# A head pair's keys, queries and values in one transfer each, and key remainders written across the halves

## The chip, the cores and the metric

One core of one Trainium2 chip runs one program. The metric is its device time in microseconds (us). The core has a matrix engine (PE, whose weight loads are shown as PEld), a vector engine (DVE), a scalar engine (ACT), GpSimd (POOL), and SyncE (SP), which here only issues transfers to one hardware queue that 16 DMA engines serve. Every engine works through its own instructions in order.

## The reference

Attention with a local window of 96 positions, 8 global keys and a linear distance bias, for 4 batches of 8 heads, 768 positions and width 64; then a two-layer block on 3072 tokens whose activation is h·cos(h). All in fp32.

```python
scores = scale * np.matmul(q, k.transpose(0, 1, 3, 2))          # q, k, v: 4 x 8 x 768 x 64
scores = np.where(keep, scores + bias, -1e9)                    # keep: last 96 positions, or the first 8 keys
a = np.exp(scores - scores.max(-1, keepdims=True))
a = a / (a.sum(-1, keepdims=True) + 1e-9)
x = np.matmul(a, v)                                             # then 3072 x 512
h = x @ w_in                                                    # 512 x 2048
return (h * np.cos(h)) @ w_out                                  # 2048 x 512
```

## The kernel before

The sequence is cut into blocks of 96 positions. A part is two to four such blocks of one batch: two parts of four blocks for the first batch, and parts of three, three and two blocks for each of the other three batches, 11 in all. A unit is one pair of heads of one part, so there are 44. The first eight units ("exact", parts 0 and 1) use q and k as they come: one transfer of 128 rows brings a pair (L626), the queries are scaled (L631, L633), and L676 makes the scores. The other 36 go through `plan_split`, once for each head: a number is cut into a high part that the fast matmul takes and a remainder. For that the head's 64 rows of keys and queries are brought twice, once into rows 0 to 63 and once into rows 64 to 127 of a `raw` buffer, each by its own transfer (L784). Then `qhigh` (L787, ACT) and `qrest` (L791, DVE) make both query parts on all 128 rows, `khigh` (a copy, line L308 on ACT, L310 on DVE, L312 on POOL) rounds the keys on all 128 rows, and `krest` (L801) overwrites rows 64 to 127 with the keys' remainder. So one matmul (L680) over 128 rows sums high and remainder. There are two `raw` buffers and two `qk` buffers, one per head of a pair.

The scores are folded and biased (L698, L707, DVE), go through exp (L732, ACT), are normed (L740, L743 on DVE; L760 and L765 on POOL or DVE), turned (L864, PE), copied (L308, L310, L875, L881) and multiplied with the values (L915, PE). The values of a unit come in two transfers: the blocks, 96 rows (L577), and the 8 global rows, broadcast to every block (L580); L838 makes the difference of neighbouring blocks. The products go into `xmem` as high part and remainder (L308, L963).

The two-layer block runs in steps: L998 multiplies by w_in; L1016, L1019, L1022, L1055 (L1121 in the first two parts) make h·cos(h); L1066 (L1129) and L1157 to L1169 make parts, remainders and sums; L1011 (first parts) or L1216 (others) multiplies by w_out. L1216 takes sums of w_out that were stored to DRAM earlier (L509 to L549) and are streamed back (`ws`, L1182, 256 transfers). The weights come as 64-bit words and are converted in the first 118 us (L441 to L478).

The order of everything is written by a planner in the kernel (`Plan`): each step has a cost in ns for each engine that may run it, a due time, the steps it waits for and the buffers it holds. The planner plays the whole kernel through, and always starts the ready step with the earliest due time; SP's transfers have a cost `extra` that stands for the queue's time, and SP stops issuing while more than 2.5 us of it are ahead. So a changed cost or a changed wait can re-order any engine's list. In the first 45 us of the plan it also puts idle matmuls (L1550) where it sees PE free.

Of the kernel before, what the change touches and what calls it, by code (L numbers as in the profile page):

```python
# [42 lines left out]
QS = KS + SW  # L43
# [17 lines left out]
NT, NST, NPV, NX, NV, NRAW, NQK, NRR, NG, NOO = 4, 3, 3, 3, 3, 2, 2, 3, 2, 2  # L61
# [222 lines left out]
class Net:  # L284
    def __init__(self, ctx, tc, qo, qk, qt, kt, v, lim, w_in, w_out, out):
        self.tc, self.nc = tc, tc.nc
        self.qo, self.qk, self.v, self.w_in, self.w_out, self.out = qo, qk, v, w_in, w_out, out
        self.qt, self.kt = qt, kt
        self.lims = lim
        self.B, self.S, _ = v.shape  # L290
        _, _, self.H, self.D, _ = qk.shape
# [267 lines left out]
    def plan_loads(self, n, b2):  # L559


        nc, p, D = self.nc, self.plan, self.D
        b, ts = self.parts[n]
        W = 2 * UB * D
        nb = len(ts)
        t0 = ts[0] * R
        lead = 1 if t0 == 0 else 0
        nt = 1 + nb - lead
        vs = Slot("v" if nt <= CT else "v5", lambda i: self.work.tile(
            [SLOT, CT + (i in self.plan.places["v5"]), W], F32, name="v", tag=i))  # L570
        low = lead if nb == CT else 0
        L = dict(n=n, first=t0 == 0, v=vs, nb=nb, low=low)
        src = self.v[b][:, b2 * W : (b2 + 1) * W]
        s = t0 - (1 - lead) * R

        def blocks(e):
            nc.sync.dma_start(vs.tile[:R, lead - low : lead - low + nt], src[s : s + nt * R].rearrange("(t p) d -> p t d", p=R))  # L577

        def glob(e):
            nc.sync.dma_start(  # L580
                vs.tile[R:, lead - low : nb - low], src[:G].rearrange("p (t d) -> p t d", t=1).broadcast_to([G, nb - lead, W])
            )
# [20 lines left out]
    def plan_unit(self, L, pr):  # L603
# [10 lines left out]
        early = n < len(OPEN)  # L614
# [4 lines left out]
        source = self.qo[n] if early else self.qk[(n - len(OPEN)) // len(BLOCKS), (n - len(OPEN)) % len(BLOCKS)]  # L619
        if exact:  # L620
            raw = Slot("early raw", lambda i: self.work.tile([P, QK if i == "raw0" else KS + 2 * SW], F32, name="raw", tag=i))
            src = source[2 * pr : 2 * pr + 2].rearrange("j p w -> (j p) w")
            kw = KW if early else KS
# [12 lines left out]
            ready = [p.op({ACT: 100 + wq * 420 // 384, DVE: 70 + wq * 230 // 384, POOL: 100 + wq * 390 // 384},  # L636
                          queries, [o], [raw], port=True)]
            heads = [(raw, ready)] * 2
        else:
            heads = [  # L640
                self.plan_split(source[2 * pr + j], k0, k1, wq, self.steepness(2 * pr + j)) for j in range(2)
            ]
# [19 lines left out]
        for job in jobs:  # L662
# [27 lines left out]
            ))  # L690
            so.slack = SLACK if n not in EARLY else 0
# [80 lines left out]
    def plan_split(self, src, k0, k1, wq, sc):  # L772
# [10 lines left out]
        def load(e, a):  # L783
            nc.sync.dma_start(raw.tile[a : a + D, k0 : KS + wq], src[:, k0 : KS + wq])  # L784

        def qhigh(e):
            nc.scalar.activation(qk.tile[0][:, 0, :wq], raw.tile[:, KS : KS + wq], AF.Copy, scale=sc)  # L787

        def qrest(e):
            qs = qk.tile[0]  # L790
            nc.vector.scalar_tensor_tensor(  # L791
                qs[:, 1, :wq], raw.tile[:, KS : KS + wq], sc, qs.bitcast(F32)[:, 0, :wq],
# [14 lines left out]
        q = self.chain("qhigh", p.op({ACT: 60 + wq * 350 // 384}, qhigh, loads, [raw, qk]))  # L807
        q = p.op({DVE: 70 + wq * 400 // 384}, qrest, [q], [raw, qk], port=True)
        k = self.chain("khigh", p.op(
            {ACT: 50 + w * 427 // 512, DVE: 70 + w * 265 // 512, POOL: 100 + w * 490 // 512},  # L810
            khigh, loads, [raw, qk], port=True,
        ))
        k = p.op({DVE: 70 + w * 535 // 512, POOL: 100 + w * 1125 // 512}, krest, [k], [raw, qk], port=True)
# [656 lines left out]
    def windows(self):  # L1470
# [8 lines left out]
                "tt": names("tt", NT), "st": names("st", NST), "qk": names("qk", NQK), "raw": names("raw", NRAW),  # L1479
# [9 lines left out]
        self.joined = []  # L1489
# [11 lines left out]
        self.when.pop()  # L1501
        self.xmem = self.const.tile([P, NX * 2 * self.NP * MW], F32R, name="xmem")
# [66 lines left out]
def layout(q, k, v, n_global, n_local, moe_w_in, moe_w_out):  # L1569
# [9 lines left out]
    def arrange(kt, qt, parts, kw, w):  # L1579
        qk = np.zeros((len(kt), len(parts), H, D, w), q.dtype)  # L1580
        for c, blocks in enumerate(parts):
            s0 = blocks[0] * R
            if c > 0:
                qk[:, c, :, :, :R] = kt[..., s0 - R : s0]
            for i, t in enumerate(blocks):
                s, o = t * R, (i + 1) * SLOT
                qk[:, c, :, :, o - G : o] = kt[..., :G]
                qk[:, c, :, :, o : o + R] = kt[..., s : s + R]
                qk[:, c, :, :, kw + i * R : kw + (i + 1) * R] = qt[..., s : s + R]
        return qk  # L1590
# [4 lines left out]
        qo=arrange(kt[:1], qt[:1], OPEN, KW, QK)[0],  # L1595
        qk=arrange(kt[1:], qt[1:], BLOCKS, KS, QS),
        qt=np.ascontiguousarray(qt),
        kt=np.ascontiguousarray(kt),
        v=np.ascontiguousarray(v.transpose(0, 2, 1, 3)).reshape(B, S, H * D),
        lim=np.concatenate([words(n_global).reshape(1), words(n_local).reshape(1)]),  # L1600
# [26 lines left out]
```

## Time and profile before

| what | value |
|---|---|
| device time, median of 3 runs | 683.9 us (682.43 to 684.13) |
| the profiled execution: its own time | 682.26 us |
| the profiled execution: its span (first to last instruction) | 679.8 us |
| PE, PEld, DVE, ACT, POOL busy | 662.9, 626.1, 567.7, 503.4, 372.5 us |
| granted TensorE clock, mean | 0.998 of full speed |
| moved by DMA | 136.69 MB in 86291 packets |

How to read it: the span is what the trace covers, and some 2.5 us of the run's time lie around it. Busy times of PE overlap, since its matmuls are pipelined; the wait of PEld or PE before an instruction is the better measure of what PE loses. DMA is read by the busy share of its 16 engines.

### The profile page before, as it was taken

How to read it: one execution, taken by the hardware profiler on the slowest of the kernel's cores; microseconds unless marked ns; L12 is line 12 of the kernel's file. 1: busy time of each engine (PE TensorE's matmuls, PEld its weight loads, DVE VectorE, ACT ScalarE, POOL GpSimd, SP SyncE). 2: the span in 40 equal slices, each digit the busy share in tenths (PEclk: the TensorE clock that was granted, in tenths of full speed). 3: DMA queues.
4: the chain of work that ended last, by engine and by line, in shares of the span. 5: the costliest groups of instructions: out<-in, count | busy, mean ns of one | idle time of the engine just before them, and what ended most of it. 6: DMA issues, size and time to landing. Idle time of an engine off the chain costs nothing.

```text
span 679.8 us, 17477 instructions
## 1 busy us (share of the span) xinstructions
PE 662.9 (98%) x5805; PEld 626.1 (92%) x5805; DVE 567.7 (84%) x1782; ACT 503.4 (74%) x1265; POOL 372.5 (55%) x526
## 2 busy tenths in 40 slices
PE   8998999999999999999999999999999999999995
PEld 4667999998999999999999999999999999999995
DVE  7889998989889878878889979887788988886764
ACT  7999999768786666877779769668678696673332
POOL 6675544347676646475755664555856565442301
PEclk9999999999999999999999999999999999999999
DMA  8999300053456476878778778777778877865664
GB/s 273 330 319 388 78 1 1 1 175 104 137 161 217 137 230 190 251 210 227 229 225 233 237 209 245 244 241 213 214 218 244 234 208 236 234 195 186 219 195 152
DMA packets 86291, 136.69 MB, mean 201 GB/s; under 512 B 9904, under 2 KB 33968, under 8 KB 86192
## 3 DMA queue, kind: packets, MB, share of 16 engines
q1 hardware_dynamic: 86048, 135.23, 65.1%
q8 instruction: 48, 0.79, 0.5%
q14 instruction: 51, 0.42, 0.2%
q10 hardware_dynamic: 144, 0.26, 0.1%
HBM read 118.67 MB, written 16.78 MB: 199 GB/s over the span
## 4 chain that ended last, share of the span: by engine, by line
PE 69%; ACT 12%; DVE 9%; DMA 5%; POOL 2%; issue 2%; SPq 0%; POOLq 0%; DVEq 0%; ACTq 0%
PE bank L998 30%; PE bank L1216 19%; PE bank L1011 8%; PE bank L680 5%; PE bank L915 5%; DMA raw<-in_qk_dram 2%; PE bank L864 2%; ACT raw L447 2%; ACT rr L1022 2%; ACT raw L463 1%; ACT w L308 1%; ACT tt L732 1%; DMA raw<-in_w_out_dram 1%; DVE rr L1055 1%; DMA raw<-in_w_in_dram 1%
## 5 line engine op out<-in xcount | busy, mean ns | idle before, releaser
L998 PE MATMUL bank<-xmem,w 128*128 128x256 f32 (+1 forms) x2112 | 347.2, 295 | 1.7 <-DVE rr L1055 0.9
L998 PEld LDWEIGHTS bank<-xmem,w 128*128 128x128 f32 x2112 | 294.6, 188 | 10.8 <-DVE rr L1121 1.6
L732 ACT ACTIVATE tt<-tt,st 96x104 f32<-96x104 f32 (+1 forms) x256 | 94.7, 371 | 13.1 <-DVE st L707 12.6
L1022 ACT ACTIVATE rr<-rr,half_pi 128x512 f32<-128x512 f32 (+1 forms) x104 | 72.2, 694 | 38.9 <-DVE rr L1019 38.4
L1011 PE MATMUL bank<-w,gh 128*128 128x256 f32 (+1 forms) x384 | 87.9, 319 | 0.0
L1016 ACT ACTIVATE rr<-bank 128x512 int32<-128x512 f32 (+1 forms) x104 | 58.3, 561 | 26.3 <-PE bank L998 26.1
L1216 PE MATMUL bank<-ws,sh 128*128 128x256 f32 x384 | 77.1, 285 | 0.3 <-DVE oo L1235 0.2
L1019 DVE SCALAR_TENSOR_TENSOR rr<-rr,bank 128x512 f32<-128x512 int32 (+1 forms) x104 | 66.2, 638 | 7.1 <-ACT rr L1016 7.0
L765 POOL TENSOR_TENSOR tt<-tt,st 96x416 f32<-96x416 f32 (+1 forms) x60 | 45.1, 758 | 41.6 <-DVE qk L791 12.4
L1055 DVE TENSOR_TENSOR rr<-bank,rr 128x512 f32<-128x512 f32 x72 | 49.5, 687 | 19.6 <-ACT rr L1022 19.2
L1011 PEld LDWEIGHTS bank<-w,gh 128*128 128x128 f32 x384 | 62.5, 188 | 1.0
L1011 PE MATMUL bank<-w,gl 128*128 128x256 f32 (+1 forms) x192 | 61.1, 318 | 0.0
L1216 PEld LDWEIGHTS bank<-ws,sh 128*128 128x128 f32 x384 | 58.5, 188 | 1.2 <-DVE oo L1235 0.6
L801 POOL TENSOR_TENSOR qk<-raw,qk 64x304 fp32r<-64x304 f32 (+1 forms) x53 | 46.6, 886 | 21.9 <-DVE qk L791 9.5
L707 DVE CUSTOM_DVE_ANT_0 tt<-bank,dd 96x104 f32<-96x104 f32 (+1 forms) x256 | 55.8, 257 | 3.0
L1216 PE MATMUL bank<-ws,sl 128*128 128x256 f32 x192 | 54.1, 282 | 0.9 <-DVE sl L1169 0.9
L308 ACT CAST sh<-sf 128x512 fp32r<-128x512 f32 x40 | 24.8, 619 | 37.1 <-DVE sf L1162 28.7
L680 PE MATMUL bank<-qk 128*96 128x200 f32 (+1 forms) x384 | 50.5, 257 | 1.0 <-POOL qk L801 0.7
L312 POOL TENSOR_SCALAR gh<-rr 128x384 fp32r<-128x384 f32 (+1 forms) x40 | 22.1, 552 | 52.3 <-DVE sf L1162 36.9
L457 POOL TENSOR_SCALAR raw<-raw 128x256 bf16<-128x256 bf16 (+1 forms) x31 | 32.5, 1065 | 32.7 <-DVE gl L1129 9.5
L1216 PE MATMUL bank<-w,gh 128*128 128x256 f32 x256 | 48.7, 281 | 0.0
L698 DVE COPY_PREDICATED bank<-mine,bank 96x192 f32<-96x192 uint32 (+1 forms) x128 | 40.4, 328 | 9.6 <-PE bank L680 8.0
(137 smaller groups left out, 1600.4 us busy)
## 6 DMA issues: line engine op xcount, KB each, us to landing
ws<-sum SPq DMA_DIRECT2D x256, 256.0 KB
raw<-in_qk_dram SPq DMA_DIRECT2D x48, 174.0 KB
raw<-in_w_in_dram SPq DMA_DIRECT2D x16, 512.0 KB
sum<-sw SPq DMA_DIRECT2D x64, 128.0 KB
raw<-in_qk_dram SPq DMA_DIRECT2D x48, 150.0 KB
raw<-in_qk_dram SPq DMA_DIRECT2D x48, 148.0 KB
out_dram<-oo SPq DMA_DIRECT2D x23, 256.0 KB
raw<-in_w_out_dram SPq DMA_DIRECT2D x16, 256.0 KB
```

The costliest lines, as they stand in the source:

```text
L680: nc.tensor.matmul(out, qs[:, m, q0], ks[:, k : k + w], start=m == 0, stop=m == 1)
L707: nc.vector.tensor_tensor_reduce(tt[t // 2].tile[:, t % 2, j, :w], ps.tile[:R, i * WIN : i * WIN + w], self.dd[:, v, :w], op0=ALU.add, op1 ...
L732: nc.scalar.activation(x, x, AF.Exp, bias=st.tile[:, c : c + 1], scale=-1.0, accum_out=st.tile[:, n2 + c : n2 + c + 1])
L765: self.eng(e).tensor_tensor(x, x, r.broadcast_to([R, na, SLOT]), op=ALU.mult)
L801: self.eng(e).tensor_tensor(ks[D:, k0:k1], raw.tile[D:, k0:k1], ks.bitcast(F32)[D:, k0:k1], op=ALU.subtract)
L998: self.nc.tensor.matmul(ph, self.wi[f][:, w, kk * P : (kk + 1) * P], xx[:, kk, :], start=kk == 0 and m == 0, stop=kk == self.NK - 1 and m ...
L1011: self.nc.tensor.matmul(out, gg, w[:, i, :], start=start and m == 0 and h == 0, stop=stop and m == 2)
L1016: self.nc.scalar.activation(r.bitcast(I32), ph, AF.Copy, scale=1.0 / TWO_PI, bias=0.25)
L1019: self.nc.vector.scalar_tensor_tensor(r, r.bitcast(I32), -TWO_PI, ph, op0=ALU.mult, op1=ALU.add)
L1022: self.nc.scalar.activation(r, r, AF.Sin, bias=self.half_pi)
L1055: {DVE: dve(512)}, lambda e: nc.vector.tensor_tensor(r(), h(), r(), op=ALU.mult), [o], [ph, rr],
L1216: nc.tensor.matmul(out, x, y, start=q == 0 and j == 0 and half == 0, stop=q == self.NF // 2 - 1 and j == 2 and ends)
```

## The change

The split units take their keys and queries from two new arrays. `ks` holds the keys of a pair, head 0 in rows 0 to 63 and head 1 in rows 64 to 127, and one transfer brings it into one of two key buffers. `qs` holds the queries of both heads, each already doubled over the halves, and one transfer brings it into the only query buffer. `khigh` now works on the head's own 64 rows; `krest` reads these rows and writes the remainder into the other 64. For the second head of a pair the high part therefore stands in rows 64 to 127 and the remainder in rows 0 to 63, and `khigh` is marked `apart` there, which adds 113 ns in the plan where it, or the step after it, follows another step directly on DVE or POOL. All these buffers and the first of the exact units' are views of one tile, so the split loads wait for all exact scores (`self.early`). The values come from `vb`, which holds 96 rows and the 8 global rows of every block, in one transfer of 104 rows. The planner's costs of these transfers change with them.

```diff
-        L["lv"] = [
-            p.op({SP: 470}, blocks, [], [vs], extra=290 * nt),
-            p.op({SP: 470}, glob, [], [vs], extra=46 * nb),
-        ]
+            nc.sync.dma_start(vs.tile[:, lead - low : lead - low + nt], src[:, s : s + nt])
+
+        L["lv"] = [p.op({SP: 470}, blocks, [], [vs], extra=150 * nt)]
...
+            if exact:
+                self.early.append(so)
...
-        raw = Slot("raw", lambda i: self.work.tile([P, QK if i == "raw0" else QS], F32, name="raw", tag=i))
+        kraw = Slot("kraw", lambda i: self.raw[:, int(i[1:]) * KS : (int(i[1:]) + 1) * KS])
+        qraw = Slot("qraw", lambda i: self.raw[:, 2 * KS : QS].rearrange("p (j w) -> p j w", j=2))
+
+        def kload(e):
+            nc.sync.dma_start(kraw.tile[:, k0:k1], self.ks[at][:, k0:k1])
+
+        def qload(e):
+            nc.sync.dma_start(qraw.tile[:, :, :wq], self.qs[at][:, :, :wq])
+
+        k = p.op({SP: 470}, kload, self.early, [kraw], extra=1500 * (k1 - k0) // 1000)
+        q = p.op({SP: 470}, qload, self.early, [qraw], extra=3000 * wq // 1000)
+        return [self.plan_head(j, kraw, qraw, k, q, k0, k1, wq, self.steepness(2 * pr + j)) for j in range(2)]
+
+    def plan_head(self, j, kraw, qraw, kload, qload, k0, k1, wq, sc):
+
+        nc, p, D = self.nc, self.plan, self.D
+        mine, other = slice(j * D, (j + 1) * D), slice((1 - j) * D, (2 - j) * D)
...
-        def load(e, a):
-            nc.sync.dma_start(raw.tile[a : a + D, k0 : KS + wq], src[:, k0 : KS + wq])
-
...
-            self.copy(e, qk.tile[1][:, k0:k1], raw.tile[:, k0:k1])
+            self.copy(e, qk.tile[1][mine, k0:k1], kraw.tile[mine, k0:k1])
...
-                ks[D:, k0:k1], raw.tile[D:, k0:k1], ks.bitcast(F32)[D:, k0:k1], op=ALU.subtract
+                ks[other, k0:k1], kraw.tile[mine, k0:k1], ks.bitcast(F32)[mine, k0:k1], op=ALU.subtract
...
-        loads = [p.op({SP: 470}, lambda e, a=a: load(e, a), [], [raw], extra=711 * (KS + wq - k0) // 1000) for a in (0, D)]
...
+        k.apart = j == 1
...
-                "tt": names("tt", NT), "st": names("st", NST), "qk": names("qk", NQK), "raw": names("raw", NRAW),
+                "tt": names("tt", NT), "st": names("st", NST), "qk": names("qk", NQK), "kraw": names("k", 2), "qraw": ["q0"],
...
+        self.raw = self.work.tile([P, QS], F32, name="raw")
```

KS is 408 (96 + 3·104), SW is 288 (3·96), and QS becomes 2·(408 + 288).

## Rows read from the trace of the kernel before

**Rows 1.** The page: busy times, and the granted clock in 40 slices (tenths).
```profile
PE 662.9 (98%) x5805; PEld 626.1 (92%) x5805; DVE 567.7 (84%) x1782; ACT 503.4 (74%) x1265; POOL 372.5 (55%) x526
...
PEclk9999999999999999999999999999999999999999
```
**Rows 2.** Busy time by stage: stretch, length, engines, clock, DMA share, GB/s.
```profile
0.00:63.00 63.00, 56.88 (x542) 39.42 (x543) 54.49 (x262) 57.15 (x195) 42.25 (x80) 1.00 0.95 322
...
160.00:673.00 513.00, 509.36 (x4671) 495.79 (x4669) 424.28 (x1331) 362.38 (x879) 283.56 (x394) 1.00 0.71 213
```
**Rows 3.** What PEld waited for, 63 to 673 us: in total, times, longest.
```profile
PEld bank L1216 <- DVE sl L1169: 1.5, 3, 0.7
PEld bank L680 <- POOL qk L801: 1.3, 3, 0.6
...
PEld bank L998 <- PE bank L864: 1.0, 2, 0.8
...
PEld bank L864 <- POOL tt L765: 0.2, 1, 0.2
```
**Rows 4.** The chain of waits, 462 to 484 us: start, length, what.
```profile
465.75 4.72 DMA raw<-in_qk_dram
...
471.18 0.84 POOL qk L801
...
477.58 0.94 PE bank L998 x6
```
**Rows 5.** Split loads by tile: issues, ns min/median/max; who waited, us and times.
```profile
L784 SPq DMA_DIRECT2D raw<-in_qk_dram x144: 465/530/1568, 63.2 to 585.7; - x144
...
  POOL qk L312: 2.5, 1
```
**Rows 6.** Value loads by tile: the same columns.
```profile
L577 SPq DMA_DIRECT2D v<-in_v_dram x44: 313/334/1097, 2.7 to 586.3; - x44
L580 SPq DMA_DIRECT2D v<-in_v_dram x44: 278/366/995, 3.8 to 586.9; - x44
...
  POOL vd L838: 8.9, 4
```
**Rows 7.** The page's packets, and DMA issues: out<-in, count, KB each.
```profile
DMA packets 86291, 136.69 MB, mean 201 GB/s; under 512 B 9904, under 2 KB 33968, under 8 KB 86192
...
raw<-in_qk_dram SPq DMA_DIRECT2D x48, 174.0 KB
```
**Rows 8.** Key conversions by tile: count, ns min/median/max, first and last start.
```profile
L801 POOL TENSOR_TENSOR qk<-raw,qk x53: 823/839/1286, 132.1 to 600.8; 64x304 fp32r<-64x304 f32 x48, 64x408 fp32r<-64x408 f32 x5
L312 POOL TENSOR_SCALAR qk<-raw x37: 440/445/657, 147.2 to 597.6; 128x304 fp32r<-128x304 f32 x25, 128x408 fp32r<-128x408 f32 x12
L308 ACT CAST qk<-raw x35: 428/447/542, 110.6 to 597.9; 128x304 fp32r<-128x304 f32 x23, 128x408 fp32r<-128x408 f32 x12
L801 DVE TENSOR_TENSOR qk<-raw,qk x19: 577/581/742, 178.1 to 546.0; 64x408 fp32r<-64x408 f32 x19
```
**Rows 9.** What SP waited for, 140 to 680 us: in total, times, longest.
```profile
SPq L1182 <- PE bank L1216: 137.8, 148, 2.8
SPq L784 <- DVE qk L791: 43.7, 24, 5.3
```
**Rows 10.** DVE's instructions in order of time, 339 to 343 us: start, length.
```profile
339.75 0.61 DVE L1158 TENSOR_TENSOR sf<-rr 128x128 f32<-128x128 f32 x1
340.29 0.28 DVE L1159 TENSOR_TENSOR sf<-sf,rr 128x128 f32<-128x128 f32 x1
340.60 0.58 DVE L801 TENSOR_TENSOR qk<-raw,qk 64x408 fp32r<-64x408 f32 x1
341.21 0.17 DVE L740 TENSOR_SCALAR st<-st 96x6 f32<-96x6 f32 x1
```
**Rows 11.** POOL's instructions in order of time, 52 to 62 us: start, length, wait.
```profile
56.76 0.72 POOL L478 TENSOR_TENSOR w<-wu,w 128x256 fp32r<-128x256 f32 x1 [2.85 <-ACT w L308]
```

**Rows 12.** PE's instructions in order of time, 60 to 63 us: start, length.
```profile
62.19 0.34 PE L915 MATMUL bank<-pv,vd 96*64 96x96 f32 x4
```

More of the change, by code (lines that the diff above doesn't have):

```diff
@@ L42 @@
 KS = R + ST * SLOT
-QS = KS + SW
+QS = 2 * (KS + SW)
 BIG = 1.0e30
@@ L59 @@
 PHASES = [(0, 0, 4), (1, 0, 16), (0, 4, 16)]
[L61 removed]
+NT, NST, NPV, NX, NV, NQK, NRR, NG, NOO = 4, 3, 3, 3, 3, 2, 3, 2, 2
 EXACT = 8
@@ L284, with __init__ @@
 class Net:
-    def __init__(self, ctx, tc, qo, qk, qt, kt, v, lim, w_in, w_out, out):
+    def __init__(self, ctx, tc, qo, ks, qs, qt, kt, v, vb, lim, w_in, w_out, out):
         self.tc, self.nc = tc, tc.nc
-        self.qo, self.qk, self.v, self.w_in, self.w_out, self.out = qo, qk, v, w_in, w_out, out
-        self.qt, self.kt = qt, kt
+        self.qo, self.ks, self.qs, self.v, self.vb = qo, ks, qs, v, vb
+        self.qt, self.kt, self.w_in, self.w_out, self.out = qt, kt, w_in, w_out, out
         self.lims = lim
         self.B, self.S, _ = v.shape
-        _, _, self.H, self.D, _ = qk.shape
+        _, self.H, self.D, _ = qt.shape
         self.DF, self.DM = w_out.shape
@@ L618, in plan_unit @@
         wq = nb * R
-        source = self.qo[n] if early else self.qk[(n - len(OPEN)) // len(BLOCKS), (n - len(OPEN)) % len(BLOCKS)]
         if exact:
-            raw = Slot("early raw", lambda i: self.work.tile([P, QK if i == "raw0" else KS + 2 * SW], F32, name="raw", tag=i))
-            src = source[2 * pr : 2 * pr + 2].rearrange("j p w -> (j p) w")
-            kw = KW if early else KS
+            raw = Slot("early raw", lambda i: self.raw if i == "raw0" else self.work.tile(
+                [P, KS + 2 * SW], F32, name="raw", tag=i))
+            src = self.qo[n][2 * pr : 2 * pr + 2].rearrange("j p w -> (j p) w")
+            kw = KW
             def load(e):
@@ L639, in plan_unit @@
         else:
-            heads = [
-                self.plan_split(source[2 * pr + j], k0, k1, wq, self.steepness(2 * pr + j)) for j in range(2)
-            ]
+            heads = self.plan_split(divmod(n - len(OPEN), len(BLOCKS)) + (pr,), pr, k0, k1, wq)
         st = u["st"] = Slot("st", lambda i: self.work.tile([R, 6 * CT], F32, name="st", tag=i))
@@ L801, in krest @@
             self.eng(e).tensor_tensor(
-                ks[D:, k0:k1], raw.tile[D:, k0:k1], ks.bitcast(F32)[D:, k0:k1], op=ALU.subtract
+                ks[other, k0:k1], kraw.tile[mine, k0:k1], ks.bitcast(F32)[mine, k0:k1], op=ALU.subtract
             )
-        loads = [p.op({SP: 470}, lambda e, a=a: load(e, a), [], [raw], extra=711 * (KS + wq - k0) // 1000) for a in (0, D)]
         w = k1 - k0
-        q = self.chain("qhigh", p.op({ACT: 60 + wq * 350 // 384}, qhigh, loads, [raw, qk]))
-        q = p.op({DVE: 70 + wq * 400 // 384}, qrest, [q], [raw, qk], port=True)
+        q = self.chain("qhigh", p.op({ACT: 60 + wq * 350 // 384}, qhigh, [qload], [qraw, qk]))
+        q = p.op({DVE: 70 + wq * 400 // 384}, qrest, [q], [qraw, qk], port=True)
         k = self.chain("khigh", p.op(
             {ACT: 50 + w * 427 // 512, DVE: 70 + w * 265 // 512, POOL: 100 + w * 490 // 512},
-            khigh, loads, [raw, qk], port=True,
+            khigh, [kload], [kraw, qk], port=True,
         ))
-        k = p.op({DVE: 70 + w * 535 // 512, POOL: 100 + w * 1125 // 512}, krest, [k], [raw, qk], port=True)
+        k.apart = j == 1
+        k = p.op({DVE: 70 + w * 535 // 512, POOL: 100 + w * 1125 // 512}, krest, [k], [kraw, qk], port=True)
         k.apart = True
@@ L1488, in windows @@
         self.weight, self.saved, self.stored = {}, {}, {}
-        self.joined = []
+        self.joined, self.early = [], []
         p = self.plan
@@ L1577, in layout, with keys @@
     kt, qt = k.transpose(0, 1, 3, 2), q.transpose(0, 1, 3, 2)
[L1579 to L1590, printed above, removed]
+    def keys(kt, blocks):
+        s0 = blocks[0] * R
+        k = np.zeros(kt.shape[:-1] + (R + len(blocks) * SLOT,), q.dtype)
+        if s0:
+            k[..., :R] = kt[..., s0 - R : s0]
+        for i, t in enumerate(blocks):
+            o = (i + 1) * SLOT
+            k[..., o - G : o] = kt[..., :G]
+            k[..., o : o + R] = kt[..., t * R : (t + 1) * R]
+        return k
+    qo = np.zeros((len(OPEN), H, D, QK), q.dtype)
+    for c, blocks in enumerate(OPEN):
+        qo[c, :, :, :KW] = keys(kt[0], blocks)
+        qo[c, :, :, KW:] = qt[0][..., c * CW : (c + 1) * CW]
+    ks = np.zeros((B - 1, len(BLOCKS), H // 2, 2 * D, KS), q.dtype)
+    qs = np.zeros((B - 1, len(BLOCKS), H // 2, 2, D, 2, SW), q.dtype)
+    for c, blocks in enumerate(BLOCKS):
+        k = keys(kt[1:], blocks)
+        ks[:, c, :, :, : k.shape[-1]] = k.reshape(B - 1, H // 2, 2 * D, -1)
+        x = qt[1:, :, :, blocks[0] * R : (blocks[-1] + 1) * R].reshape(B - 1, H // 2, 2, D, -1)
+        qs[:, c, :, :, :, :, : x.shape[-1]] = x.transpose(0, 1, 3, 2, 4)[:, :, None]
+    rows = v.transpose(0, 2, 1, 3).reshape(B, S // R, R, H // 2, 2 * D).transpose(0, 3, 2, 1, 4)
+    vb = np.zeros((B, H // 2, SLOT, S // R, 2 * D), q.dtype)
+    vb[:, :, :R] = rows
+    vb[:, :, R:] = rows[:, :, :G, :1]
     nk, nf = moe_w_in.shape[0] // P, moe_w_in.shape[1] // P
@@ L1594, in layout @@
     return dict(
-        qo=arrange(kt[:1], qt[:1], OPEN, KW, QK)[0],
-        qk=arrange(kt[1:], qt[1:], BLOCKS, KS, QS),
+        qo=qo,
+        ks=ks,
+        qs=qs.reshape(B - 1, len(BLOCKS), H // 2, 2 * D, 2, SW),
         qt=np.ascontiguousarray(qt),
```

17 lines of the change are left out of this document (6 added, 11 removed).

## The prediction

> **What bounds the kernel now.** I read the page first. PE is busy for 98% of the span at full clock throughout [rows 1], so the question is only where PE still loses time. Busy shares hide that, because matmuls overlap; the stages by PEld say more. From 160 to 673 us the weight loads are busy 495.8 of 513 us, while in the first 63 us they are busy 39.4 of 63 us, with ACT at 57.2 and DVE at 54.5 us [rows 2]. So there are two regimes: an opening in which ACT and DVE work on the first eight units and the weights, and a long stretch in which PE sets the pace. In that stretch the list of what PEld waited for has 13 entries, which add up to 8.8 us; the first is 1.5 us, the last 0.2 us [rows 3]. No entry names a DMA. That is the first thing to see: nothing that the change shortens stands directly before PE.
>
> Indirectly it does. One chain of waits starts with a split load, issued at 465.75 us and under way for 4.72 us, goes through the second head's conversion on POOL, and ends at a matmul at 477.58 us [rows 4] before which PEld had waited 0.8 us (the longest of the two waits behind L864 [rows 3]). POOL itself stood 2.5 us for that load [rows 5]. The three waits of the scores (L680) for `krest` on POOL cost 1.3 us together [rows 3].
>
> **The change, part by part.**
>
> Issues. 144 split loads of 0.53 us become 72 [rows 5], and 44 of the 88 value loads go, at 0.37 us [rows 6]: 72 x 0.53 + 44 x 0.37 = 54 us less of SP's time, if a 128-row issue costs what a 64-row one does; at the longest issue of either kind, 1.57 us [rows 5], 72 of them would take 113 us against the 76 us of the 144, and SP would spend some 20 us more. I take the first, since the issue of the value load's 96 rows is no longer than that of its 8 rows [rows 6]. SP is not on PE's path, so this is worth nothing by itself.
>
> Bytes. In a part of three blocks with a block before it, a pair brings four times 174 KB [rows 7], that is 696 KB; after it 128 rows x 408 columns x 4 bytes = 204 KB of keys and 128 x 576 x 4 = 288 KB of queries, 492 KB, 29% less. The values bring as many bytes, in runs of 1.5 to 2.5 KB per row instead of 512 B, so much of the 24 thousand packets between 512 B and 2 KB [rows 7] becomes fewer and larger ones. The DMA engines are busy 95% in the opening and 71% later [rows 2]; both should fall. What this gives PE is bounded by what waited for these loads: POOL 2.5 us for keys and 8.9 us for values [rows 5, 6], of which PE lost at most the 0.8 us above and the part of the 8.8 us that lies behind POOL. The values' 8.9 us end at `vd`, well ahead of L915, and no entry of PEld leads back to them, so I take nothing for them.
>
> The Trainium skill, "DMA: Bandwidth & Descriptors", section "Why a DMA increments its semaphore by 16 and not by 1", says that a transfer is spread over the largest number of engines up to 16 that divides its slowest dimension; by that 104 rows go over 13 engines where 96 rows went over 16. No row here shows a 104-row transfer. By it a value load's bytes would take 16/13 of their time, which would eat part of the gain of longer runs, and the time would be that of the rival "hidden anyway" below.
>
> Conversions. Their number stays: 72 `qhigh`, 72 `qrest`, 72 `khigh` (37 on POOL, 35 on ACT) and 72 `krest` (53 on POOL, 19 on DVE) [rows 8]. `khigh` loses half its rows and no column; a 64-row subtraction of 408 columns on DVE takes 0.58 us [rows 8], and a 128-row one of 128 columns 0.28 us [rows 10], so columns and not rows set the length and I take no gain. Writing into the other half is not in the trace. Below, a gain has no reason, since columns stay; above, a doubled `krest` on POOL would add 53 x 0.84 = 45 us to an engine that is busy 284 of 513 us [rows 2]. I take zero, the value of the in-place row.
>
> On DVE a step that starts at another row has a price in the trace: L1159 starts 0.07 us before L1158 ends, but `krest`, which starts at row 64, starts 0.03 us after its predecessor's end, and its successor 0.03 us after its own [rows 10]. So each such step costs about 0.1 us on either side, paid 19 times now. `krest` keeps that price. `khigh` of the second head takes it on only where the plan puts it on DVE, and now none of the 72 is there [rows 8]. The Trainium skill, "VectorE: DVE Perf Modes", section "Two Vector instructions with no wait between them", states the rule: an instruction whose inputs or output start in another group of 32 partitions than the last ones waits for all earlier ones. These rows agree, and by the rule 36 such copies on DVE would be the last rival below.
>
> Waits. Split loads wait for all exact scores. The first split load is issued at 63.2 us [rows 5], after the last exact unit, so the wait is over before it matters, and it costs nothing unless the plan wants such a load before 50 us. The keys have two pair-wide buffers, but the queries one, so a query load waits for both `qrest` of the pair before. SP already stands behind `qrest` for 43.7 us in 24 waits [rows 9]. Queued behind it are the `ws` stream, value loads and stores. The stream's cover is its depth: it waits for PE to free a buffer 148 times [rows 9], and PE never waits for it. Without that cover the longest such wait, 5.3 us, could reach PE.
>
> Order. The planner's costs of the loads fall, from 290 to 150 ns per value block for example, and all lists are laid anew. For that I have no row; its bounds are taken from single events of the lists as they are: one badly placed step costs 2.85 us on POOL in the opening [rows 11], and all waits of the long stretch are 8.8 us. I take zero with both signs open.
>
> The sum. Both heads' data now arrive together, so I let the four waits that lead back to loads and conversions go: 1.3 + 0.8 = 2.1 us. Next late is DVE: the remaining waits, 6.7 us, are mostly for sums, remainders and products on it, and stay. On the profiled execution's own time that is 682.26 - 2.1 = 680.2 us; the median of the runs lies 1.6 us above that execution, so against 683.9 us I predict **681.8 us**. Around it, the forecast's own range goes from 680.0 us (double the gain) to 683.5 us (a fifth of it). A change of under 0.3%, 2.05 us, can hardly be told from none here.
>
> **Rivals.**
> *The opening gets shorter too.* The DMA engines are full there [rows 2], and with shorter value loads weights arrive earlier. If the new order loses the 2.85 us for which POOL stood behind a weight step ahead of the last norms of part 1 [rows 11], the time is 681.8 - 2.9 = 678.9 us. Against it: ACT and DVE are themselves near full there, and they do the same work.
> *Hidden anyway.* The four waits stay, because DVE's work ahead of them is late as well (the chain ends in L1055, not in a conversion [rows 4]), or the loads come no sooner: 683.9 us.
> *The order turns out worse.* One mechanism: in the opening an in-order engine is given a weight step whose input is late, ahead of the norms of part 1, once more than now. The price is one more such stand, 2.85 us [rows 11]: 686.8 us. It decides from the point at which the last product of part 1 (L915) ends later than now, at 62.5 us [rows 12]. For it speaks that every cost in the plan shifts; against, that shorter loads give the plan more room.
> *DVE pays for the halves.* If the plan puts the second heads' `khigh` on DVE, 36 x 0.2 = 7 us more of its time; DVE is busy 424 of 513 us [rows 2], so perhaps a third reaches PE: 686.2 us.
>
> **How the numbers follow.** Chances: the forecast 0.42, the shorter opening 0.17, hidden anyway 0.17, the worse order 0.18, DVE 0.06. The forecast lies at the edge of what can be told: I put 0.25 of its 0.42 beyond 0.3%. Faster is then 0.25 + 0.17 = 0.42, the same 0.17 + 0.17 = 0.34, slower 0.18 + 0.06 = 0.24. The range reaches from about a microsecond below the shorter opening, 677.8 us, to just above the worse order, 687.1 us, and leaves out the outer halves of these two and the doubled `krest`.
>
> **What would show it.** Right: two transfers per pair and one per unit for values, fewer packets, a lower DMA share, `krest` at 0.58 us on DVE and 0.84 us on POOL as now; no wait of POOL or ACT for a key load after 160 us, and L680's waits for L801 gone; PEld's waits after 63 us near 6.7 us. The first 63 us tell the two order rivals apart: when the last L915 of part 1 ends. Wrong: `krest` longer, `khigh` on DVE, a PE wait for `ws`, or a sum of waits that moves by more than 3 us in spells that hold no load at all.

## The result, and the profile after

| | median of the runs | ratio to the kernel before, 95% interval | span of the profiled execution |
|---|---|---|---|
| before | 683.83 us (682.43 to 684.13) | 1 | 679.8 us |
| after | 689.46 us (688.81 to 690.45) | 1.0088 (1.0069 to 1.0106) | 687.5 us |

The change makes the kernel 5.6 us slower. The forecast was 681.8 us, and the time lies above the range, which ended at 687.1 us. The profiled execution of after took 689.19 us of its own time, against 682.26 us.

The page of after has PE's busy time, clock and packets as follows; it answers to [rows 1] and [rows 7].

```profile
PE 665.3 (97%) x5803; PEld 630.4 (92%) x5803; DVE 561.5 (82%) x1747; ACT 504.9 (73%) x1267; POOL 390.0 (57%) x553
...
PEclk9998999999999999999999999999999999999999
...
DMA packets 74893, 129.33 MB, mean 188 GB/s; under 512 B 8268, under 2 KB 26636, under 8 KB 74796
```

One digit of the clock, the fourth, is new: from 51.6 to 68.7 us (slices of 17.2 us) PE had less than full speed. Busy time by stage (columns as in [rows 2]) says the same from the other side:

```profile
0.00:63.00 63.00, 50.96 (x451) 34.98 (x453) 50.99 (x250) 54.58 (x193) 44.81 (x79) 0.95 0.98 330
160.00:673.00 513.00, 509.96 (x4653) 496.20 (x4653) 421.20 (x1311) 364.32 (x890) 297.69 (x423) 1.00 0.64 196
```

In the long stretch PEld is as busy as before (496.2 against 495.8 us). In the opening it does 35.0 us in 63 where it did 39.4 [rows 2]. A finer cut, first of before, then of after:

```profile
50.00:55.00 5.00, 4.53 (x53) 3.67 (x50) 4.96 (x20) 4.94 (x13) 2.83 (x4) 1.00 0.95 325
55.00:60.00 5.00, 3.39 (x26) 3.07 (x25) 4.22 (x10) 4.98 (x13) 2.55 (x4) 1.00 1.03 400
60.00:65.00 5.00, 4.73 (x53) 4.32 (x53) 5.00 (x10) 4.63 (x11) 3.07 (x3) 1.00 1.04 408
```
```profile
50.00:55.00 5.00, 2.07 (x15) 1.28 (x15) 4.58 (x27) 4.03 (x17) 4.67 (x8) 1.00 1.05 277
55.00:60.00 5.00, 0.84 (x5) 0.84 (x6) 3.81 (x11) 4.97 (x15) 2.68 (x3) 0.64 1.03 395
60.00:65.00 5.00, 5.00 (x46) 4.29 (x46) 2.73 (x6) 3.72 (x9) 3.08 (x3) 0.68 1.04 397
...
57.00:63.00 6.00, 3.84 (x18) 3.29 (x20) 4.36 (x10) 5.35 (x11) 4.41 (x5) 0.50 1.03 398
```

From 50 to 60 us PE was busy 2.9 us in place of 7.9. The granted clock fell: its means of 0.64 and 0.68 mix two levels, and from 57 to 63 us it stood at the lower one (0.50, that is 1.2 GHz; 1.00 is 2.4 GHz), where before had 1.00 throughout. What PE waited for is in its instructions in order of time (start, length, and in brackets the idle time and what ended it). The last line is the last product of part 1, which answers to [rows 12]:

```profile
59.16 0.88 PE L868 MATMUL bank<-ident,tt 96*104 96x96 f32 x4 [5.80 <-POOL tt L756]
...
68.45 0.34 PE L919 MATMUL bank<-pv,vd 96*64 96x96 f32 x4
```

So one turn (L868, in the kernel before L864) waited 5.8 us for POOL's norm (L756, in the kernel before L765), and part 1 ended at 68.8 us, not at 62.5. POOL and DVE in that spell, of after:

```profile
53.67 0.76 POOL L457 TENSOR_SCALAR raw<-raw 128x256 bf16<-128x256 bf16 x1
54.25 0.41 POOL L465 TENSOR_SCALAR raw<-raw 128x256 f32<-128x256 f32 x1
54.63 1.33 POOL L457 TENSOR_SCALAR raw<-raw 128x512 bf16<-128x512 bf16 x1
58.23 1.72 POOL L756 TENSOR_TENSOR tt<-tt,st 96x416 f32<-96x416 f32 x2 [2.27 <-DVE wu L468]
```
```profile
56.97 0.17 DVE L734 RECIPROCAL st<-st 96x4 f32<-96x4 f32 x1
57.06 0.41 DVE L468 SCALAR_TENSOR_TENSOR wu<-raw 128x256 uint32<-128x256 uint32 x1
57.39 0.15 DVE L714 TENSOR_TENSOR worst<-worst,st 96x8 f32<-96x8 f32 x1
57.46 0.68 DVE L468 SCALAR_TENSOR_TENSOR wu<-raw 128x512 uint32<-128x512 uint32 x1
```

POOL ran three weight steps in a row until 55.96 us and then stood 2.27 us. The norm begins 0.09 us after DVE's second weight step (L468, ends 58.14 us), not after the last of the reciprocals (57.14 us). The reason is in the kernel: the planner calls some DVE steps `port` and lets no POOL step run beside them, so its plan keeps the two apart in time, and the written program holds a POOL step behind the DVE `port` step planned ahead of it. This is read from the kernel and these lines; no run took that hold alone away.

To see where each order loses, I counted the matmuls begun by a time, gave each the interval it has where PE runs without a gap at 2.4 GHz (0.1745 us for 128x384, 0.2325 us for 128x512, 0.117 us for 128x256, and so on; idle products count nothing), and subtracted that sum from the time. The differences between the rows are what counts; they are good to some tenths of a us. The rows below the first two are experiments, told further down.

```
PE time lost by       50 us   70 us  150 us  170 us  200 us  300 us  640 us
before                 23.2    27.3    28.4    30.6    32.3    35.5    51.6
after                  23.4    33.9    34.4    36.8    39.1    43.2    59.3
new value numbers      23.1    33.2    33.3    35.6    37.3    41.4    63.6
and value transfer     23.9    34.7    34.9    37.2    38.6    42.6    69.4
old value numbers      23.0    27.2    28.4    31.1    32.7    37.7    52.6
idle products          24.8    33.6    34.2    36.7    39.0    42.9    58.6
no port                24.2    30.4    32.6    38.4    39.7    44.0    59.2
no port, filled        24.3    30.0    32.1    37.9    39.2    43.5    58.3
DEFER 5000             23.0    29.8    31.0    36.8    38.1    43.4    58.7
DEFER 5000, filled     23.1    27.6    28.9    36.3    37.5    42.0    57.4
value number 230       24.0    29.2    30.1    32.8    34.5    39.1    53.4
230, filled            23.5    27.7    28.5    31.3    32.9    37.6    52.1
last sign step on DVE  23.1    33.5    34.7    37.1    39.6    43.5    58.9
```

Between before and after 6.6 us (33.9 - 27.3) arise by 70 us, nearly all of them after 50 us. By 640 us it is 7.7 us, which is also the difference of the two spans. The medians differ by less, 5.6 us; the profiled execution of before was 1.6 us faster than its median.

### The profile page after: what moved, and what is told of

Read it like the earlier page. It is cut to its first block, busy times and chain, and to the rows that moved or that the text cites. A ratio compares the mean times of both kernels' runs of the same rounds, so it can differ in the third digit from the quotient of the medians.

```text
span 687.5 us, 17224 instructions
## 1 busy us (share of the span) xinstructions
PE 665.3 (97%) x5803; PEld 630.4 (92%) x5803; DVE 561.5 (82%) x1747; ACT 504.9 (73%) x1267; POOL 390.0 (57%) x553
## 4 chain that ended last, share of the span: by engine, by line
PE 69%; ACT 3%; DVE 2%; POOL 1%; issue 1%; POOLq 0%; ACTq 0%; DVEq 0%
PE bank L1002 31%; PE bank L1220 21%; PE bank L1015 6%; PE bank L669 5%; PE bank L919 4%; PE bank L868 2%; ACT tt L723 1%; DVE rr L1059 0%; ACT L1026 0%; ACT qk L308 0%; DVE sl L1173 0%; ACT rr L1026 0%; ACT L723 0%; DVE st L731 0%; ACT qk L791 0%
## 5 line engine op out<-in xcount | busy, mean ns | idle before, releaser
L756 POOL TENSOR_TENSOR tt<-tt,st 96x416 f32<-96x416 f32 (+1 forms) x60 | 45.6, 767 | 39.7 <-DVE sw L531 6.4
L805 POOL TENSOR_TENSOR qk<-raw,qk 64x304 fp32r<-64x304 f32 (+1 forms) x56 | 52.4, 936 | 20.8 <-DVE worst L714 7.0
L457 POOL TENSOR_SCALAR raw<-raw 128x512 bf16<-128x512 bf16 (+1 forms) x35 | 38.1, 1099 | 34.3 <-DVE w L478 11.8
L669 PE MATMUL bank<-qk 128*96 128x200 f32 (+1 forms) x384 | 51.6, 258 | 1.9 <-POOL tt L751 0.8
L308 ACT CAST gh<-rr 128x384 fp32r<-128x384 f32 (+1 forms) x68 | 34.9, 513 | 24.6 <-PE bank L1220 10.2
L312 POOL TENSOR_SCALAR gh<-rr 128x384 fp32r<-128x384 f32 (+1 forms) x36 | 19.4, 538 | 57.5 <-DVE sf L1166 39.1
L669 PEld LDWEIGHTS bank<-qk 128*96 128x96 f32 x384 | 43.5, 162 | 5.4 <-POOL qk L805 3.1
```

What stands on the lines that cost most here:

```text
L669: nc.tensor.matmul(out, qs[:, m, q0], ks[:, k : k + w], start=m == 0, stop=m == 1)
L756: self.eng(e).tensor_tensor(x, x, r.broadcast_to([R, na, SLOT]), op=ALU.mult)
L805: self.eng(e).tensor_tensor(ks[other, k0:k1], kraw.tile[mine, k0:k1], ks.bitcast(F32)[mine, k0:k1], op=ALU.subtract)
```

## The experiments

Each ratio is to executions of the kernel before taken beside that experiment. Their medians were 683.05 us (first four experiments), 683.93 us (next four) and 683.25 us (last four), so times from different groups compare only to about 0.9 us.

**Numbers or transfers: four kernels.** The first is the kernel before with nothing but the planner's numbers for the values as the change has them, its transfers untouched.

```diff
-            p.op({SP: 470}, blocks, [], [vs], extra=290 * nt),
-            p.op({SP: 470}, glob, [], [vs], extra=46 * nb),
+            p.op({SP: 470}, blocks, [], [vs], extra=150 * nt),
+            p.op({SP: 0}, glob, [], [vs], extra=0),
```

> The kernel before, with nothing changed but two numbers in the plan: a value load of nt blocks is told at 150 ns per block and its global rows at nothing (before: 290 per block, 46 per block for the global rows, 470 of SP). All transfers and steps are those of before. Order theory: the whole loss comes from the order that the plan writes for the first 63 us, and these two numbers alone bring it about, so the time is 688 to 690 us, PE stands some 5 to 6 us before L864 between 53 and 60 us, and the granted clock falls there. Transfer theory (the 104-row value transfer or the key and query transfers are what costs): 683 to 684.5 us, as before.

Measured: 694.0 us, ratio 1.0158 (1.0138 to 1.0177), 4 us above what was expected. The second has the change's single value transfer as well, in the same order, and the keys and queries of before.

```diff
+            nc.sync.dma_start(vs.tile[:, lead - low : lead - low + nt], src[:, s : s + nt])
+
+        L["lv"] = [p.op({SP: 470}, blocks, [], [vs], extra=150 * nt)]
```

> The kernel before with the value part of the change alone: values of a unit in one transfer of 104 rows, at the new plan cost. Its order on every engine is the one of the run with the new numbers only; the one difference is the transfer itself. Order theory: 688 to 690 us, within 1 us of that run. Transfer theory: if 104 rows are slow to land, longer than that run by several us and POOL's wait for values over the 8.9 us of before; if they land sooner, that wait falls to 2 us or less, and the time stays.

Measured: 699.63 us, ratio 1.0232 (1.0184 to 1.0279), 5.6 us above the first and not within 1 us of it. The third is the change with the two value transfers of before and their numbers.

```diff
-        L["lv"] = [p.op({SP: 470}, blocks, [], [vs], extra=150 * nt)]
+        L["lv"] = [
+            p.op({SP: 470}, blocks, [], [vs], extra=290 * nt),
+            p.op({SP: 470}, glob, [], [vs], extra=46 * nb),
+        ]
```

> The changed kernel with the values as before (two transfers, old plan cost): keys and queries in one transfer each, remainders across the halves. Its order up to the first split unit is that of before. Order theory: the opening is that of before (last L919 of part 1 ends at 62 to 63 us), the time 682.5 to 685.5 us. Theory that writing across the halves or the single query buffer costs: 687 us or more, with a longer krest or waits of PE behind it after 140 us.

Measured: 682.65 us, ratio 0.9996 (0.9983 to 1.0009). The fourth is the whole change with its single transfer, but the planner is told the old numbers by means of an empty second step.

```diff
-        L["lv"] = [p.op({SP: 470}, blocks, [], [vs], extra=150 * nt)]
+        L["lv"] = [
+            p.op({SP: 470}, blocks, [], [vs], extra=290 * nt),
+            p.op({SP: 470}, nothing, [], [vs], extra=46 * nb),
+        ]
```

> The changed kernel with all its transfers and steps, but the plan is told the old cost of the value loads (290 ns per block, and a second SP step of 470 ns that issues nothing). Its order on PE, ACT, DVE and POOL is the one of the run with keys and queries only. Order theory: 682.5 to 685.5 us, within 1 us of that run, so that the change's parts on the chip cost nothing and the 5.6 us are the plan's. Theory that the value transfer of 104 rows costs on the chip: slower than that run by 2 us or more.

Measured: 682.46 us, ratio 0.999 (0.9978 to 1.0003). The turn of part 1, first in the kernel before with new numbers, then in the change with old ones:

```profile
57.92 0.88 PE L864 MATMUL bank<-ident,tt 96*104 96x96 f32 x4 [5.79 <-POOL tt L765]
```
```profile
58.23 0.54 PE L874 MATMUL bank<-ident,tt 96*104 96x96 f32 x4 [1.62 <-POOL tt L762]
```

PE's wait of 5.8 us comes with the numbers, without any part of the change that runs on the chip, and goes with them, though all of that part is there. Up to 108 us the first kernel's lists on PE, ACT, DVE and POOL are those of after, and by 70 us it has lost 33.2 us against 33.9. With the old numbers the change is worth -0.6 us, which can't be told from nothing; the single value transfer (fourth against third, same order on the four engines) is worth -0.2 us there.

The new numbers cost more in the kernel before, 11 us, and 16.6 us with the value transfer: from 300 to 640 us these two lose 22.2 and 26.8 us, before and after 16.1 each. What the first loses there I did not follow. The second runs the first's lists on these four engines, instruction by instruction, so its further 5.6 us (four runs each, 693.66 to 694.37 and 695.61 to 702.23 us) go with the value transfer. The largest piece lies between 540 and 560 us (4.2 us lost against 1.1):

```profile
553.89 0.56 DVE L830 TENSOR_TENSOR vd<-v 96x384 f32<-96x384 f32 x1 [1.60 <-DMA v<-in_vb_dram]
```
```profile
556.36 0.67 PE L1208 MATMUL bank<-ws,sh 128*128 128x256 f32 x2 [1.87 <-DVE oo L1227]
```

DVE waits 1.60 us for values that arrive late; behind it come a remainder on DVE, an output step on POOL and one on DVE, and PE waits 1.87 us for that, with the granted clock at 0.91 from 540 to 560 us. So the single transfer is not free in every order. POOL's wait for values before `vd` in the one traced execution of each, of the third and the fourth kernel, then of the first and the second (us, times):

```profile
  POOL vd L850: 0.2, 1
```
```profile
  POOL vd L848: 1.8, 2
```
```profile
  POOL vd L838: 8.5, 4
```
```profile
  POOL vd L830: 11.1, 4
```

So in the same order POOL waited longer for the single transfer than for the two, both times.

**How much of it is the clock.** The change with idle products also in the stands that the plan sees up to 62 us, which keep PE from being idle there; the order is the same.

```diff
-FILL_TO, FILL_REST, FILL_EACH, FILL_FIRST, FILL_COLD = 45000, 150, 250, 10, 7000
+FILL_TO, FILL_REST, FILL_EACH, FILL_FIRST, FILL_COLD = 62000, 150, 250, 10, 7000
```

> The changed kernel with idle matmuls also between 45 and 62 us of the plan (21 more in the hole of PE ahead of the last norms of part 1); every list is otherwise that of the changed kernel. It parts the two shares of the hole. If the hole costs by the wait itself and, behind it, by matmuls at a granted clock of about 0.6 between 56 and 64 us, the clock stays at 1.00, and the time falls by the second share alone, 1.5 to 2.5 us, to 687 to 688 us. If the clock is not part of it: 689 to 690 us.

Measured: 687.51 us, ratio 1.0059 (1.0038 to 1.0079). Its busy time in the two stretches that had 0.64 and 0.68:

```profile
55.00:60.00 5.00, 4.53 (x21) 1.86 (x19) 4.07 (x20) 4.97 (x17) 2.63 (x5) 1.00 1.02 381
60.00:65.00 5.00, 4.28 (x52) 3.81 (x53) 3.96 (x7) 4.54 (x11) 4.60 (x5) 1.00 1.03 401
```

The median fell by 2.0 us, as the clock theory had it. By 70 us PE is only 0.3 us further (33.6 against 33.9), but this execution was 1.4 us behind by 50 us (24.8 against 23.4), before the first added idle product at 52.23 us, and POOL's norm came as much later, after the same wait for the same step:

```profile
59.78 1.72 POOL L756 TENSOR_TENSOR tt<-tt,st 96x416 f32<-96x416 f32 x2 [2.25 <-DVE wu L468]
```

From 50 to 70 us it lost 8.8 us where after lost 10.5. So the clock's share of the 5.6 us is about 2 us (1.7 by this count, 2.0 by the medians), and most of the loss is the wait.

**Taking the wait away.** First the exclusion: the opening's add and reciprocal of the exact units may run beside POOL.

```diff
-                o = p.op({DVE: 85}, lambda e, cs=cs: add(e, *cs), ends, [st], port=True)
-                o = p.op({DVE: 120}, lambda e, cs=cs: rec(e, *cs), [o], [st], port=True)
+                o = p.op({DVE: 85}, lambda e, cs=cs: add(e, *cs), ends, [st], port=not exact)
+                o = p.op({DVE: 120}, lambda e, cs=cs: rec(e, *cs), [o], [st], port=not exact)
```

> The changed kernel, but the two small DVE steps (add and reciprocal of four columns) ahead of the norms of the first eight units are no longer told to the plan as steps that cannot run beside POOL. In the plan of the changed kernel the reciprocal stands 2.3 us behind three weight steps on POOL, the norm behind it, and PE has 5.5 us without work. Theory that this exclusion, and the order it makes, is the mechanism: no PE hole over 3 us in 40 to 65 us, the last L919 of part 1 ends at 63 us or before, time 682 to 685.5 us. Theory that the early arrival of weights crowds the engines in any order: the hole stays near 5 us or moves, 688 to 690 us.

Measured: 689.51 us, ratio 1.0082 (1.0054 to 1.0109): no gain, and inside the rival's range. Then one constant of the planner, by which a step that needs its engine's last step counts as due later.

```diff
-    DEFER = 4000
+    DEFER = 5000
```

> The changed kernel with one other number in the plan: a step that would follow its own predecessor directly on DVE or POOL is put off by 5000 instead of 4000 ns of due time. The plan comes out 3.0 us shorter than that of the changed kernel (662.1 against 665.1 us; before 662.0), its last product of part 1 at 56.5 instead of 61.0 us. Theory that the loss is an accident of the order and nothing in the changed transfers: 680 to 684 us. Theory that transfers or halves cost: 687 us or more.

Measured: 688.71 us (684.24 to 691.57), ratio 1.0051 (1.0014 to 1.0089). In both the long wait is gone (PEld's longest waits for POOL's norm from 40 to 70 us are 1.1 and 2.0 us; in after it was 6.1), and by 150 us they have lost 1.8 and 3.4 us less than after. By 170 us that is given back, at the first turn of part 2. PE's line for it in the one and in the other, and the clock behind it (columns as in [rows 2]):

```profile
161.37 0.86 PE L868 MATMUL bank<-ident,tt 96*96 96x96 f32 x4 [2.34 <-POOL tt L751]
...
160.00:165.00 5.00, 3.38 (x21) 2.83 (x21) 3.32 (x10) 4.27 (x8) 3.63 (x7) 0.86 0.21 59
165.00:170.00 5.00, 5.00 (x43) 4.62 (x43) 4.14 (x23) 3.98 (x10) 2.83 (x4) 0.80 0.18 47
```
```profile
159.48 0.86 PE L868 MATMUL bank<-ident,tt 96*96 96x96 f32 x4 [2.29 <-POOL tt L751]
...
160.00:165.00 5.00, 4.96 (x25) 4.47 (x26) 3.30 (x12) 3.15 (x8) 4.42 (x7) 0.66 0.24 75
```

So neither gain came, for one reason: the edit took the wait away by making another order, and that order has its own. From 150 to 170 us each of the two loses 5.8 us, after 2.4 and before 2.2. The rivals' reasons (weights that crowd the engines in any order, transfers or halves that cost) don't hold: with old numbers the same transfers and halves lose 27.2 us by 70 us, before 27.3.

**Another number.** The change with 230 ns for each value block, between the old 290 and the new 150.

```diff
-        L["lv"] = [p.op({SP: 470}, blocks, [], [vs], extra=150 * nt)]
+        L["lv"] = [p.op({SP: 470}, blocks, [], [vs], extra=230 * nt)]
```

> The changed kernel, told 230 ns per value block in place of 150. The plan is 662.4 us long and puts the last product of part 1 at 55.2 us. Theory of the order: 680 to 684 us, and a last L919 of part 1 that ends at 60 us or before. Theory that transfers or halves cost: 687 us or more.

Measured: 684.17 us, ratio 1.0001 (0.9988 to 1.0014), just above the 680 to 684 us expected. The transfers are those of the change, and 5.3 us are gone. The last product of part 1 ends at 61.4 us, and by 70 us it has lost 29.2 us, 1.9 more than before, by 200 us 2.2 more.

**The clock again, in the other orders.** The three orders with idle products in the planned stands, up to 175 us (DEFER 5000 and no port) or 62 us (230 ns), the edit being that of `FILL_TO` above.

> The changed kernel with the planning constant DEFER at 5000 as in the run before, and idle products put into TensorE's planned stands up to 175 us in place of 45 us. The order stays that of the run before. Clock theory: there the granted clock stood at 0.82 (52 to 56 us, 2.42 us busy), 0.50 (56 to 60, 4.00 busy) and 0.83 (60 to 64, 4.00 busy), and at 0.66 from 160 to 165 us (4.96 busy): 0.4 + 2.0 + 0.7 + 1.7 = 4.8 us of TensorE's work lost; with the clock held the time falls from 688.7 to 683.5 to 685 us, with granted clocks of 1.00 in these windows, while the waits for POOL of 2.0 us in the opening and of 2.7 us near 157 us stay. Rival, that the clock falls where TensorE would have waited anyway: 688 to 690 us.

Measured: 686.25 us (684.61 to 687.49), ratio 1.004 (1.0022 to 1.0058): 2.5 us less than without, or 1.8 if each is held against its own executions of before, where the clock theory had put 3.7 to 5.2. The two intervals overlap, so by the times alone this gain isn't sure. By 70 us it is 2.2 us ahead of the unfilled order (27.6 against 29.8), with the clock at 1.00 from 48 to 64 us; by 170 us 0.5 us are left. There the idle products did not hold the clock, against what was expected; it is 0.66 as without them:

```profile
160.00:165.00 5.00, 5.00 (x27) 4.71 (x27) 3.60 (x14) 3.94 (x9) 4.46 (x7) 0.66 0.20 54
```

What waits there is a chain over four engines, ACT, DVE, POOL and PE in turn:

```profile
156.61 0.78 ACT L791 ACTIVATE qk<-raw 128x288 fp32r<-128x288 f32 x2 [1.75 <-DMA raw<-in_qs_dram]
```
```profile
157.09 0.83 DVE L795 SCALAR_TENSOR_TENSOR qk<-raw,qk 128x288 fp32r<-128x288 f32 x2 [1.40 <-ACT qk L791]
157.83 0.42 DVE L509 TENSOR_TENSOR sw<-sw 128x256 f32<-128x256 f32 x1
```
```profile
158.42 0.99 POOL L751 TENSOR_TENSOR tt<-tt,st 96x192 f32<-96x192 f32 x2 [4.33 <-DVE sw L509]
```
```profile
158.98 0.87 PE L868 MATMUL bank<-ident,tt 96*96 96x96 f32 x4 [1.62 <-POOL tt L751]
```

A query transfer that arrives late holds `qhigh`, that holds `qrest`, behind which DVE has a weight sum (L509), and POOL's norm is written behind that sum. The norm itself needs none of these. In the unfilled order the same norm began at 158.92 us, and ACT stood 0.17 us for that transfer. So PE was 2.1 us ahead by 150 us (28.9 against 31.0), and the norm came 0.5 us earlier.

> The changed kernel with the opening's add and reciprocal not exclusive against POOL, as in the run before, and idle products in TensorE's planned stands up to 175 us. Clock theory: that run had 0.80 (52 to 56 us, 3.21 us busy), 0.50 (56 to 60, 3.60 busy), 0.85 (60 to 64, 4.00 busy), 0.86 (160 to 165, 3.38 busy) and 0.80 (165 to 170, 5.00 busy): 0.6 + 1.8 + 0.6 + 0.5 + 1.0 = 4.5 us lost; with the clock held the time falls from 689.5 to 684 to 686 us. Rival, that the clock falls where TensorE would have waited anyway: 688.5 to 690.5 us.

Measured: 689.89 us, ratio 1.0107 (1.0081 to 1.0132): nothing gained, though the clock was 1.00 in every stretch named. PE's loss by 70 us is 30.0 us against 30.4. Here the rival holds: the clock fell while PE would have waited anyway.

> The changed kernel with the value transfer told at 230 ns for each block, as in the run before, and idle products in TensorE's planned stands up to 62 us. Clock theory: that run had 0.66 from 50 to 55 us with 4.95 us busy, 1.7 us lost; with the clock held the time falls from 684.2 to 682 to 683 us, which would be the lowest of the changed kernel's orders and 1 us under the kernel before. Rival: 684 to 684.5 us.

Measured: 681.93 us (681.69 to 683.19), ratio 0.9987 (0.9978 to 0.9996). The stretch from 50 to 55 us, without and with idle products:

```profile
50.00:55.00 5.00, 4.95 (x32) 4.52 (x32) 3.93 (x20) 3.50 (x18) 3.12 (x4) 0.66 1.03 356
```
```profile
50.00:55.00 5.00, 4.66 (x53) 3.65 (x53) 4.96 (x23) 4.68 (x18) 2.35 (x3) 1.00 1.03 355
```

Here 32 matmuls began at 0.66 of the clock and 53 (idle ones among them) at 1.00, the loss by 70 us falls from 29.2 to 27.7 us, nothing later takes it back (53.4 and 52.1 by 640 us), and the time falls by 2.2 us, or 1.6 held against the executions of before beside each. This is the lowest median of the changed kernel, 1.3 us under the kernel before by an interval that excludes 1, though within the 0.3% that this text counts as no change.

**One step off POOL.** The sign step of the last quarter of the output weights, the longest of POOL's three (1.33 us), may be planned on DVE alone.

```diff
-        o = p.op({DVE: part(650), POOL: part(1310)}, wsign, [o], [raw], port=True)
+        o = p.op({DVE: part(650)} if place in ("wo3",) else {DVE: part(650), POOL: part(1310)}, wsign, [o], [raw], port=True)
```

> The changed kernel, but the sign step of the last quarter of the output weights, the longest of the three weight steps that POOL runs between its two norms in the opening, may be planned on DVE alone. Theory that these steps hold back the reciprocal and the norm, and with them TensorE's turn: the 6.1 us wait for POOL's norm near 54 us is shorter by about the step's 1.3 us or more, the clock's fall with it, and the time falls from 689.5 to 685.5 to 688.5 us. Rival, that the wait is set by VectorE, which gets the step and is no freer than POOL: the wait stays at 5 us or more and the time at 689 to 691 us.

Measured: 688.35 us, ratio 1.0076 (1.0056 to 1.0095). PE's two turns in its opening:

```profile
55.23 0.88 PE L868 MATMUL bank<-ident,tt 96*104 96x96 f32 x4 [2.86 <-POOL tt L756]
...
58.17 0.88 PE L868 MATMUL bank<-ident,tt 96*104 96x96 f32 x4 [2.06 <-POOL tt L756]
```

The wait of 5.80 us became two of 2.86 and 2.06 us: 0.9 us of the wait went, and 1.1 us of the time (0.5 held against the executions of before beside each). This fits a step that held back the norm, but the order on DVE and POOL is another from 54.6 us on, and what holds the rest was not tried step by step.

## Why the prediction was wrong

**What bounds the kernel** was read rightly: PE sets the pace from 160 to 673 us, and that stretch stayed as it was. What was given too little weight is that the opening is where an order can lose, since PE there hangs on norms that share two in-order engines with the weights.

**Issues and bytes** held. The loads of after by tile (columns as in [rows 5, 6]):

```profile
L770 SPq DMA_DIRECT2D raw<-in_ks_dram x36: 328/333/550, 64.0 to 583.6; - x36
...
L773 SPq DMA_DIRECT2D raw<-in_qs_dram x36: 327/352/667, 62.8 to 591.1; - x36
...
L577 SPq DMA_DIRECT2D v<-in_vb_dram x44: 308/343/1317, 2.7 to 594.4; - x44
...
  POOL vd L842: 1.5, 3
```

72 split loads at a median of 0.33 and 0.35 us (0.53 before) and 44 for values at 0.34 (0.33 and 0.37); POOL's wait for values fell from 8.9 to 1.5 us, and no engine waits for a key load. The value transfer is not what shortened that wait: the third kernel, which has the new key and query loads and the old value transfers, has 0.2 us. DMA's share of the long stretch fell from 0.71 to 0.64; in the opening, where the prediction had it fall too, it rose from 0.95 to 0.98. From 140 to 680 us SP stood 19.4 us behind `qrest` for the single query buffer (43.7 before for `raw` [rows 9]), and no PEld wait leads to `ws`. All this was worth nothing on PE, as the prediction said of each. The Trainium skill, "DMA: Bandwidth & Descriptors", section "Why a DMA increments its semaphore by 16 and not by 1", would have the 104-row load run over 13 engines, which the prediction turned into an estimate of 16/13 of the time. No view here names the engines of a transfer. The runs show that it cost no time in one order (-0.2 us) and 5.6 us in another, and that in both POOL waited longer for it than for the two transfers; whether the engines are the reason is not shown.

**Conversions** held at zero: `krest`, which now crosses the halves, and its unchanged length on both engines, of after, against [rows 8]:

```profile
L805 POOL TENSOR_TENSOR qk<-raw,qk x56: 824/840/2378, 138.0 to 608.5; 64x304 fp32r<-64x304 f32 x48, 64x408 fp32r<-64x408 f32 x8
...
L805 DVE TENSOR_TENSOR qk<-raw,qk x16: 577/578/732, 179.3 to 553.2; 64x408 fp32r<-64x408 f32 x16
```

The bound of 45 us for a doubled step fell away, and no `khigh` went to DVE, so that rival did not come about.

**Waits**: the forecast's own term was 2.1 us for four waits that were to go. Of PEld's waits from 63 to 673 us, of after, two lines answer to [rows 3]:

```profile
PEld bank L669 <- POOL qk L805: 3.1, 7, 1.2
...
PEld bank L1002 <- PE bank L868: 0.9, 2, 0.5
```

The scores' waits for `krest` did not go; they grew from 1.3 to 3.1 us, though no load stands behind them any more. All PEld waits of the stretch fell from 8.8 to 7.4 us, not to 6.7. With the old numbers the whole term was -0.6 us, with zero in its interval: "hidden anyway" was the right rival for what the change does on the chip.

**Order** is the step that failed. It was taken at zero with the sign open, and as a rival it had the right sign: an in-order engine given weight steps ahead of part 1's norms, deciding from a last product later than 62.5 us. That product ended at 68.8 us. The price was mis-sized: 2.85 us, one stand of POOL [rows 11], where the wait that reached PE was 5.80 us and the loss by 70 us 6.6 us. The mechanism was half right: the stand of [rows 11] was one of a weight step whose input is late, while here POOL ran three weight steps without a gap, and then the norm was held behind a DVE weight step by the `port` rule. Behind the wait PE worked at the lower clock, about 2 us more, for which the prediction had no term. The chance of 0.18 was also low for a change whose edits on the chip were all put near zero: then the order is all that is left, and the lists were said to be laid anew.

**What stays open**: what the new numbers cost in the kernel before after 300 us; and why the single value transfer arrives late in one order and does no harm in another. Whether the wait at the first turn of part 2 could be taken away by itself was not tried.

## What to carry to other kernels

Where a kernel's order is worked out from costs, try the costs alone first: put the new numbers into the old kernel and the old numbers into the new one. Here the two told an effect of 5.6 us apart from an edit worth -0.6 us. An edit's worth belongs to its order, too: the value transfer was worth -0.2 us in one and cost 5.6 us in another. A wait that one order shows is no property of the code: taking it away by a constant or a rule makes another order, so compare how much work the bound engine has done by a given time, and further on, before a gain is counted.

## What the runs showed of the hardware

In after PE began no product from 53.4 to 59.2 us, and the granted clock was at its lower level (0.50, 1.2 GHz) from 57 to 63 us. Idle matmuls held it at 1.00 in the opening of four orders, but not from 160 to 165 us of one (0.66). What that is worth depends on what PE has ready: by 70 us 2.2 and 1.5 us in two orders, 1.7 us from 50 to 70 us in a third, and 0.4 us in a fourth, in which PE got little further with the full clock. And writing a result to 64 rows other than those of its inputs costs `krest` nothing: 840 ns against 839 on POOL, 578 against 581 on DVE.
